# A long convolution with routed experts: channels in four parts of 32, first transform on two row groups, products by halves of a step, z read by whole chunks

## The chip, the cores and the metric

The kernel runs on one core of a Trainium2 chip. What counts is the device time of one execution in microseconds (us). A profile of one execution is at hand, with every instruction, every transfer and the clock that TensorE was granted.

The engines are named as the profile names them: PE (TensorE's products; PEld its weight loads), DVE (VectorE), ACT (ScalarE), POOL (GpSimd) and SP (SyncE, which only issues transfers here). Each engine works through its own instructions in the order in which they were written.

## The reference

For 4 sequences of 11456 positions and 128 channels, `u = x * v` is convolved along the positions with a filter that a small network makes from position vectors. The result times x goes through a layer of eight experts, of which each row that passes a score takes one.

```python
h_filt = (np.maximum(pos_emb @ w1, 0.0) @ w2) * np.exp(-0.01 * pos)[:, None]
Uf, Hf = np.fft.rfft(x * v, n=2 * S, axis=1), np.fft.rfft(h_filt, n=2 * S, axis=0)
x = x * np.fft.irfft(Uf * Hf[None], n=2 * S, axis=1)[:, :S, :]
...
out[do_compute] = xc + gate_w * (np.maximum(xc @ w1[e], 0.0) @ w2[e])
```

## The kernel before

The positions are cut into 3 blocks of 3840 = 60 x 64, and the transform of each block is done in steps of products with fixed matrices, all in float32. Between the steps the data goes to DRAM and comes back in another order. There are three stages.

**Stage 1** (`first_phase`) does the first transform, over 60 positions, for the first half of the channels (64 of 128), and builds the filter's transform beside it. `First.load` (L189) brings a piece of x and one of v in runs of 1 KB, `mult` (L207) multiplies them on DVE, `split` (L211) makes two fp32r halves of the product on ACT and DVE, `data` (L219) multiplies them with c1 in three passes (L204), ACT copies the result out of PSUM (L205), and ACT's queue stores it in `x1d` (L239). Two sets of 60 positions stand below each other on 120 partitions; c1 holds two 120 x 120 matrices, each with zeros in the half that belongs to the other set. `filt` (L244) is a generator whose pieces are woven in; it ends in products with c1f (L290) and in stores to `x1d` from POOL (L298).

**Stage 2** (`freq_phase`) has 60 steps: two halves of channels times 30 steps of 2 frequencies. A step loads `x1` (L397) and its matrices c2 (L395). `filt` (L400) transforms the filter (L403), ACT copies it out (L409), and DVE (L410) and POOL (L411) make combinations of its blocks. `forward` (L414) does the second transform of the data in three blocks (L428, 2 x 256 columns each) and multiplies each out of PSUM with the filter on DVE (L422, six of 1024 elements a step) into y and p; POOL adds these (L424, three of 1024). `back` (L452) takes y of the step two before (`LAG`) through the third transform (L455, six products of 512 columns), ACT copies it to z (L456), and SP stores z in `zd` (L460). After each `back`, `step` (L382) may write a piece of the first transform of the other half of the channels (`second`, L371). In all a step has 3 x 2 x 256 + 2 x 192 + 6 x 512 = 4992 columns on PE without these pieces.

**Stage 3** (`out_phase`) has 32 chunks of 3 blocks. A block loads x (L1049) and its 480 KB of z (L1060) and takes them through the last transform (`product`, L1063). There the two products of one block (L1071) have 64 columns of weights each and write partitions 0 to 63 and 64 to 127. DVE multiplies by x (L1072), and scores, tables and gathers for the experts follow. The rows are gathered into 16 buffers (`XT`), and the experts' products fill PE to the end (`late_slots`).

What sets the order: each stage is written with its schedule fixed, so an engine's order is the order in which the Python code runs. SP issues transfers strictly in that order, and each waits for its buffer and for an earlier transfer that used the same one of eight semaphores.

In the second half of stage 2 `prepare` (L1319) sets up the experts a piece at a time and loads their weights. Its first piece has a copy on DVE of `slotpos` into four buffers (L539) as soon as its load has landed.

Of the kernel before, what the change touches and what calls it, by code (L numbers as in the profile page):

```python
# [20 lines left out]
E, F = 8, 1024  # L21
# [6 lines left out]
DH = D // 2  # L28
# [13 lines left out]
AHEAD = 1  # L42
LEAD = 3
PIECES = 1.2
FSTART = 2
FEND = 2
QX = 4
# [5 lines left out]
ZT = 4  # L53
XT = 16
GATHERS = 12
FETCH = 5
# [17 lines left out]
def tables():  # L74
# [6 lines left out]
    c1 = np.zeros((2, K1, 2, K1, 2))  # L81
    c1f = np.zeros((64, 2, 2, K1, 2))
    for p in range(2):
        c1[p, :, p] = c1f[:K1, p, p] = np.stack([np.cos(th), -np.sin(th)], axis=-1)
# [12 lines left out]
    c3[:64, 1, :64] = -np.sin(ps)  # L97
    c3[64:, 1, :64] = -np.cos(ps)
    c3[:64, 1, 64:] = np.cos(ps)
    c3[64:, 1, 64:] = -np.sin(ps)  # L100
# [37 lines left out]
    winp = winp.transpose(1, 0, 2, 3)  # L138
    return {
        "c1": c1.reshape(2 * K1, 2, 2 * K1).astype(f), "c1f": c1f.reshape(128, 2, 2 * K1).astype(f),  # L140
        "c2": c2.astype(f), "c3": c3.astype(f),
# [14 lines left out]
class First:  # L156


    Q = 4
    STEPS = NB * N2 // (2 * Q)  # L160
    XV, US, XS = 3, 2, 3

    def __init__(self, nc, i, x1d, mc, stage):
        self.nc, self.i, self.x1d = nc, i, x1d
        n = self.Q * B * DH
        at = [0]

        def piece(k):
            at[0] += k * n
            return stage[0:2 * K1, at[0] - k * n:at[0]]  # L170
        self.xv = [[piece(1) for _ in range(self.XV)] for _ in "xv"]
        self.us = [piece(1) for _ in range(self.US)]
        self.xs = [piece(2) for _ in range(self.XS)]
        self.c1 = mc.tile([2 * K1, 2, 2 * K1], F32, name="c1")
        nc.scalar.dma_start(self.c1, i["c1"])
        self.tiles, self.loaded, self.parts = {}, 0, {}

    def halves(self, pool):
        self.c1r = pool.tile([2 * K1, 2, 2, 2 * K1], F32R, name="c1r")
        self.nc.scalar.copy(self.c1r[:, 0], self.c1)  # L180
        self.nc.vector.tensor_tensor(self.c1r[:, 1], self.c1, self.c1r[:, 0].bitcast(F32), ALU.subtract)

    def ahead(self, step):

        while self.loaded < min(step + self.XV, 2 * self.STEPS):
            self.load(self.loaded)
            self.loaded += 1

    def load(self, step):  # L189
        nc, Q = self.nc, self.Q  # L190
        h, r = divmod(step, self.STEPS)
        blk, ch = divmod(r, N2 // (2 * Q))
        self.tiles[step] = []
        for a, nm in enumerate("xv"):
            t = self.xv[a][step % self.XV]
            nc.sync.dma_start(
                t.rearrange("n (q c) -> n q c", q=Q),
                self.i[nm][ch * 2 * Q:(ch + 1) * 2 * Q, :, blk, h].rearrange("(q p) n b d -> (p n) q (b d)", p=2))
            self.tiles[step].append(t)

    def first(self, xs, terms, pool):
        ps = pool.tile([2 * K1, 512], F32, name="ps")
        for a, (c, rhs) in enumerate(terms):
            self.nc.tensor.matmul(ps, c, rhs, start=(a == 0), stop=(a == len(terms) - 1))  # L204
        self.nc.scalar.copy(xs, ps.rearrange("k (q c) -> k q c", c=B * DH))  # L205

    def mult(self, step):  # L207
        if step < 2 * self.STEPS:
            self.nc.vector.tensor_tensor(self.us[step % self.US], *self.tiles.pop(step), ALU.mult)

    def split(self, step, pool):  # L211

        u = self.us[step % self.US]
        ur = pool.tile([2 * K1, 2, self.Q * B * DH], F32R, name="ur")
        self.nc.scalar.copy(ur[:, 0], u)  # L215
        self.nc.vector.tensor_tensor(ur[:, 1], u, ur[:, 0].bitcast(F32), ALU.subtract)
        self.parts[step] = ur

    def data(self, step, pool):  # L219
        nc, Q = self.nc, self.Q  # L220
        h, r = divmod(step, self.STEPS)
        blk, ch = divmod(r, N2 // (2 * Q))
        u = self.us[step % self.US]
        xs = self.xs[step % self.XS]
        n = Q * B * DH
        ur = self.parts.pop(step, None)

        def terms(p, sl):
            if ur is None:
                return (self.c1[:, p, :], u[:, sl]),  # L230
            return [(self.c1r[:, a, p, :], ur[:, b, sl]) for a, b in ((0, 0), (0, 1), (1, 0))]
        for p in range(2):
            for hf in range(n // 512):
                sl = slice(hf * 512, hf * 512 + 512)
                qs = slice(sl.start // (B * DH), sl.stop // (B * DH))
                self.first(xs.rearrange("k (q p c) -> k q p c", q=Q, p=2)[:, qs, p], terms(p, sl), pool)
                if p or hf < n // 512 - 1:
                    yield
        nc.scalar.dma_start(  # L239
            self.x1d[h][:, :, ch * 2 * Q:(ch + 1) * 2 * Q, blk * B * DH:(blk + 1) * B * DH].rearrange("k c m d -> (k c) m d"),  # L240
            xs.rearrange("k (m c) -> k m c", c=B * DH))
        yield
# [1125 lines left out]
```

## Time and profile before

| | us |
|---|---|
| median of three runs | 1756.87 (1756.68 to 1761.15) |
| the profiled execution | 1761.34 |
| its span, first to last instruction | 1759.6 |
| PE busy | 1615.1 (92%) |
| DVE busy | 1269.8 (72%) |
| POOL busy | 1020.3 (58%) |
| ACT busy | 862.7 (49%) |

DMA moved 357.8 MB, 203 GB/s over the span. The mean granted clock of TensorE was 0.969 of full speed.

A busy share is a mean over stages with different limits, so the prediction reads the stages apart. A row of the timeline has start, length, engine, line, operation and tiles; a bracket at its end says how long the engine had been idle and what it was waiting for. float32 products stand there as two records each. A group row (with a bar) has busy time, mean ns of one, and the idle time ahead of it.

### The profile page before, as it was taken

The page shows a single profiled execution, that of the slowest core. Times are in us where ns is not written, and L with a number is a line of the kernel's source. Part 1 is how long each engine was busy: PE and PEld are TensorE (multiplying, and loading weights), DVE is VectorE, ACT ScalarE, POOL GpSimd, SP SyncE. Part 2 cuts the span into 40 slices and gives each one's busy share as a digit, 9 for nine tenths or more (in the row PEclk, how much of TensorE's full clock was granted, in tenths as well). Part 3 has the DMA queues.
Part 4 walks back from the last instruction along what each step waited for, and adds up shares of the span by engine and source line. Part 5 has one row for each costly group of instructions (what it writes and reads, how often), then busy time and mean ns, then how long its engine had stood idle before and what let it go on. Part 6 is the DMA issues. An engine that isn't in the chain of part 4 may idle for free. (4 is left out here: it accounts for less than half of the span.)

```text
span 1759.6 us, 27314 instructions
## 1 busy us (share of the span) xinstructions
PE 1615.1 (92%) x8980; PEld 1121.0 (64%) x8980; DVE 1269.8 (72%) x2404; ACT 862.7 (49%) x1582; POOL 1020.3 (58%) x767
## 2 busy tenths in 40 slices
PE   4989679999999799999567999999998999999996
PEld 2556345555556466655234677777677888888996
DVE  3334359777788799999277778767786777777885
ACT  3655435454454344443133555555544555556773
POOL 1111138677678699999002563632657777776874
PEclk9999889999999899999898999999998999999998
DMA  9999999999998599985999888998831111111110
GB/s 246 304 314 304 299 290 277 305 334 301 338 294 239 160 283 302 276 236 147 214 281 257 223 239 233 247 241 227 232 108 47 31 46 46 44 41 33 36 37 21
DMA packets 255122, 357.80 MB, mean 203 GB/s; under 512 B 24961, under 2 KB 189739, under 8 KB 254979
## 3 DMA queue, kind: packets, MB, share of 16 engines
q1 hardware_dynamic: 187692, 269.74, 53.2%
q10 hardware_dynamic: 47687, 47.71, 8.9%
q0 software_dynamic: 19600, 38.59, 8.4%
q8 instruction: 72, 1.18, 0.3%
q14 instruction: 71, 0.58, 0.1%
HBM read 212.91 MB, written 144.02 MB: 203 GB/s over the span
## 5 line engine op out<-in xcount | busy, mean ns | idle before, releaser
L424 POOL TENSOR_TENSOR y<-y,p 128x1024 f32<-128x1024 f32 x120 | 282.9, 2358 | 101.0 <-DVE y L422 96.3
L455 PE MATMUL zps<-y,c 128*128 128x512 f32 x720 | 339.6, 595 | 0.0
L767 POOL DMA_INDIRECT out<-o,ids x186 | 201.6, 1084 | 178.0 <-DVE o L773 128.5
L703 POOL DMA_INDIRECT xt<-out,ids x186 | 199.1, 1070 | 93.1 <-issue 42.5
L422 DVE TENSOR_TENSOR p<-xp,g 128x1024 f32<-128x1024 f32 x180 | 218.4, 1213 | 44.3 <-PE xp L428 27.0
L422 DVE TENSOR_TENSOR y<-xp,gc 128x1024 f32<-128x1024 f32 x180 | 218.5, 1214 | 20.9 <-PE xp L428 20.9
L428 PEld LDWEIGHTS xp<-x,c 128*128 128x128 f32 x720 | 137.6, 192 | 109.5 <-issue 77.2
L871 DVE SCALAR_TENSOR_TENSOR hh<-hp,hh 128x1024 fp32r<-128x1024 f32 x128 | 155.9, 1218 | 70.5 <-ACT hh L870 70.5
L428 PE MATMUL xp<-x,c 128*128 128x256 f32 x720 | 187.9, 384 | 14.1 <-DVE p L422 14.1
L455 PEld LDWEIGHTS zps<-y,c 128*128 128x128 f32 x720 | 134.9, 191 | 99.9 <-issue 89.7
L456 ACT COPY z<-zps 128x512 f32<-128x512 f32 x180 | 104.0, 587 | 189.2 <-PE zps L455 187.2
L669 POOL DMA_INDIRECT ids<-lists,at x93 | 102.7, 1104 | 134.5 <-DMA out<-xm 93.8
L409 ACT COPY gc<-t 64x384 f32<-64x384 f32 x240 | 113.7, 474 | 135.2 <-DVE y L422 80.1
L870 ACT ACTIVATE hh<-hp 128x1024 fp32r<-128x1024 f32 x128 | 132.1, 1032 | 74.2 <-PE hp L763 74.2
L205 ACT COPY wf<-ps 120x512 f32<-120x512 f32 x192 | 110.4, 591 | 83.4 <-PE ps L204 38.5
L738 DVE TENSOR_TENSOR ws<-wf,ws 128x1024 fp32r<-128x1024 f32 x113 | 137.8, 1220 | 18.1 <-ACT ws L733 11.8
L424 POOL TENSOR_TENSOR p<-p,p 128x1024 f32<-128x1024 f32 x60 | 149.5, 2492 | 0.0
L204 PE MATMUL ps<-ur,c1r 120*120 120x512 f32 x300 | 113.3, 508 | 37.9 <-ACT ur L215 20.4
L1071 PE MATMUL y<-zt,c 120*64 120x512 f32 x384 | 108.4, 643 | 32.0 <-DMA zt<-zd 25.9
L833 PEld LDWEIGHTS bank<-wd,h 128*128 128x128 f32 x928 | 107.8, 191 | 30.9 <-issue 30.8
L761 PE MATMUL hp<-hl,ws 128*128 128x512 f32 (+1 forms) x336 | 122.2, 364 | 2.4 <-DVE hh L871 0.9
L733 ACT CAST ws<-wf 128x1024 fp32r x113 | 117.8, 1043 | 10.4 <-issue 5.1
(194 smaller groups left out, 3330.8 us busy)
## 6 DMA issues: line engine op xcount, KB each, us to landing
x<-x1d SPq DMA_DIRECT2D x60, 960.0 KB
x1d<-wf ACTq DMA_DIRECT2D x48, 960.0 KB
zd<-z SPq DMA_DIRECT2D x120, 384.0 KB
zt<-zd SPq DMA_DIRECT2D x96, 480.0 KB
out<-xm SPq DMA_DIRECT2D x96, 258.0 KB
ox<-xo SPq DMA_DIRECT2D x96, 256.0 KB
wf<-x SPq DMA_DIRECT2D x48, 480.0 KB
wf<-v SPq DMA_DIRECT2D x48, 480.0 KB
```

Source lines behind the costliest of these rows:

```text
L409: nc.scalar.copy(gc[h * 64:(h + 1) * 64, a], t[a * 64:(a + 1) * 64])
L422: nc.vector.tensor_tensor(o, x[:, None].broadcast_to([128, 2, B, D]), v[:, :, None, :].broadcast_to([128, 2, B, D]), ALU.mult)
L424: add = lambda o, v: nc.gpsimd.tensor_tensor(o, o, v, ALU.add)
L428: nc.tensor.matmul(x[:, :, k], c2[:, k], x1[:, k, blk * B:(blk + 1) * B, :], start=True, stop=True)
L455: nc.tensor.matmul(zps, c3[:, a, :], y[:, blk, a], start=(a == 0), stop=(a == 1))
L703: ins = nc.gpsimd.indirect_dma_start(out=xt[:, j], out_offset=None, in_=self.rows[0:have], in_offset=bass.IndirectOffsetOnAxis(ap=ids[:, j ...
L733: nc.scalar.copy(w[:, 0], (self.w1f, self.w2f)[which][:, ds(self.where(nc.scalar, tb), F)])
L738: eng.tensor_tensor(w[:, 1], src[:, ds(self.where(eng, tb), F)], w[:, 0].bitcast(F32), ALU.subtract)
L761: nc.tensor.matmul(hp, w[:, 0, c], hl[:, 0], start=True, stop=False)
L767: ins = nc.gpsimd.indirect_dma_start(out=self.rows, out_offset=bass.IndirectOffsetOnAxis(ap=ids[:, j:j + 1], axis=0), in_=o, in_offset=Non ...
L870: nc.scalar.activation(h[:, 0], hp, AF.Relu)
L871: nc.vector.scalar_tensor_tensor(h[:, 1], hp, 0.0, h[:, 0].bitcast(F32), ALU.max, ALU.subtract)
```

## The change

The channels go in four parts of 32 instead of two halves of 64 (`NP`, `DH`). What follows from that and what is new beside it:

- Stage 1 does the first transform for one part only. The fp32r split is gone. One transfer brings x and v of a piece together, in runs of 6 KB, and a store of x1d writes runs of 6 KB. The two sets of 60 positions now stand on partitions 0 to 59 and 64 to 123 and are multiplied with the same 60 x 120 matrix, as two products of 384 columns with 60 rows each (L215). The filter's products use the same matrix (L267). The filter has a tensor of its own, `x1f`.
- The x1d stores are issued by SP, one step later, and no longer by ACT.
- Stage 2 has 60 steps still: four parts of 15 steps of 4 frequencies. It does the first transform of the other three parts; x times v is on POOL there (L198). A step loads x1 (L381) and the filter (L382) by two transfers. c2 is loaded once and stays.
- The second transform takes data and filter in one product of 480 columns (`spread`, L392), two halves of a step apart, each in its own PSUM tiles. DVE combines the filter out of PSUM (`combine`, L404, L405) and multiplies by halves (`mult`, L412: 1536, 1024 and 512 elements). POOL adds all in two instructions (2048 and 1024 elements, L483, L484). `LAG` is 1 instead of 2.
- z's stores are held back until after the next step's first half. Each run in `zd` has 1536 bytes instead of 3072.
- Stage 3 loads z by whole chunks (1440 KB, two buffers, `ZB`) and x with three buffers; there are 14 row buffers, 4 units of gathers ahead, and 4 buffers h. The row buffers' memsets and the copy of slotpos stand at the start of stage 3.

```diff
-DH = D // 2
+NP = 4
+DH = D // NP
...
-ZT = 4
-XT = 16
+ZT = 3
+ZB = 2
+XT = 14
...
     def mult(self, step):
-        if step < 2 * self.STEPS:
-            self.nc.vector.tensor_tensor(self.us[step % self.US], *self.tiles.pop(step), ALU.mult)
...
+            eng = self.nc.vector if step < self.STEPS else self.nc.gpsimd
+            eng.tensor_tensor(self.us[step % self.US][rows], xv[:, 0], xv[:, 1], ALU.mult)
...
+        for q in range(Q):
+            ps = [pool.tile([2 * K1, 512], F32, name="ps")[:, 0:RUN] for _ in range(2)]
+            for p in range(2):
+                rows = slice(p * 64, p * 64 + K1)
+                nc.tensor.matmul(ps[p], self.c1[rows], u[rows, q * RUN:(q + 1) * RUN], start=True, stop=True)
+            for p in range(2):
+                nc.scalar.copy(xs[:, 2 * q + p], ps[p])
+            if q == 0:
+                self.store()
...
         def step():
-            credit[0] += PIECES
+            n = fi.STEPS * fi.Q
+            credit[0] += (n - LEAD) / (NB * (PER - QX)) if done[0] < n else n / (NB * PER)
...
+            nc.sync.dma_start(x1[:, :, 0:fi.RUN], fi.x1d[h][ks].rearrange("k c n w -> (c n) k w"))
+            nc.sync.dma_start(x1[:, :, fi.RUN:], fi.x1f[ks, :, :, h * w:(h + 1) * w].rearrange("k c n w -> (c n) k w"))
...
+            xp = qpx.tile([128, KH, 512], F32, name=f"xp{j}")
+            for k in range(KH):
+                nc.tensor.matmul(xp[:, k, 0:(NS + NB) * DH], c2(n % PER * KS + j * KH + k), x1[:, j * KH + k], start=True, stop=True)
...
-        LAG = 2
+        LAG = 1
...
+                half(0)
+                combine(n, 1)
+            back(0)
+            begin(n + 1, 0)
+            store()
+            if n < ALL:
+                half(1)
+                del gs[n], xs[n]
+            back(1)
+            if n + 1 < ALL:
+                combine(n + 1, 0)
+            begin(n + 1, 1)
+            if n < ALL:
+                nc.gpsimd.tensor_tensor(y[:, 1:], y[:, 1:], p1, ALU.add)
+                nc.gpsimd.tensor_tensor(y[:, 2:], y[:, 2:], p2, ALU.add)
+            back(2)
...
-            z = ob.tile([2 * K1, 4, BW], F32, name="zt", bufs=ZT)
-            nc.sync.dma_start(z, zs[ch][:, :, blk * BW:(blk + 1) * BW])
+                zts[ch] = ob.tile([2 * K1, 2 * NP, NS * DH], F32, name="zt", bufs=ZB)
+                nc.sync.dma_start(zts[ch], zs[ch])
```

How this moves instructions is seen in the order in which they stand on each engine. On PE, a step in the first half of stage 2 stood like this before (L428 second transform of the data, L403 of the filter, L455 third, L204 first transform of the other half of the channels):

```order
L428 MATMUL xp_2355<-x_2155,c_2153 128x4x64 x2
L403 MATMUL t<-x_2222,c_2220 128x3x64 x2
L455 MATMUL zps<-y,c_61 128x512 x2
L204 MATMUL ps<-wf,c_59 120x512 x2
L428 MATMUL xp_2382<-x_2155,c_2153 128x4x64 x2
L455 MATMUL zps<-y,c_61 128x512 x2
L204 MATMUL ps<-wf,c_59 120x512
L428 MATMUL xp_2396<-x_2155,c_2153 128x4x64 x2
L455 MATMUL zps<-y,c_61 128x512 x2
```

And this is a step of the first part in the changed program (L392 second transform, L423 third, L215 first transform of another part):

```order
L392 MATMUL xp_1340<-x_1182,wf 128x480 x2
L423 MATMUL zps<-y,c_67 128x512 x2
L215 MATMUL ps<-wf,c_65 120x384 x2
L392 MATMUL xp_1363<-x_1182,wf 128x480 x2
L423 MATMUL zps<-y,c_67 128x512 x2
L215 MATMUL ps<-wf,c_65 120x384 x2
L423 MATMUL zps<-y,c_67 128x512 x2
L215 MATMUL ps<-wf,c_65 120x384 x2
```

The third transform and the second one have as many columns as before; the first transform's products come as pairs of 384 columns between them.

On SP, a step of the first half stood like this before (L395 c2, L397 x1, L196 x and v, L460 z; the stores of x1d were on ACT's queue):

```order
L395 DMA c_1889<-c 128x2x128
L397 DMA x_1891<-x1d 128x2x960
L196 DMA wf<-x 120x4x256
L196 DMA wf<-v 120x4x256
L460 DMA zd<-z 64x2x768 x2
```

In the changed program a step of the second part stands like this (L381 x1, L382 the filter, L191 x and v together, L203 the store of x1d, L434 z):

```order
L381 DMA x_2033<-x1d 128x4x384
L382 DMA x_2033<-x1f 128x4x96
L191 DMA wf<-xv 60x1536 x2
L203 DMA x1d<-wf 120x1536
L434 DMA zd<-z 64x4x384 x2
```

The queue has seven transfers a step where it had six, the stores of x1d among them, and their runs are shorter for x1, the filter and z and longer for x, v and x1d.

More of the change, by code (lines that the diff above doesn't have):

```diff
@@ L169, in piece @@
             at[0] += k * n
-            return stage[0:2 * K1, at[0] - k * n:at[0]]
-        self.xv = [[piece(1) for _ in range(self.XV)] for _ in "xv"]
+            return stage[:, at[0] - k * n:at[0]]
+        self.xv = [piece(2).rearrange("n (a c) -> n a c", a=2) for _ in range(self.XV)]
         self.us = [piece(1) for _ in range(self.US)]
-        self.xs = [piece(2) for _ in range(self.XS)]
-        self.c1 = mc.tile([2 * K1, 2, 2 * K1], F32, name="c1")
-        nc.scalar.dma_start(self.c1, i["c1"])
[L176 to L181, printed above, removed]
+        self.xs = [piece(2)[0:2 * K1] for _ in range(self.XS)]
+        self.used = at[0]
+        for xv in self.xv:
+            for rows in (slice(32, 64), slice(96, 128)):
+                nc.vector.memset(xv[rows], 0.0)
+        self.c1 = mc.tile([128, 2 * K1], F32, name="c1")
+        nc.scalar.dma_start(self.c1, i["c1"])
+        self.loaded, self.late = 0, []
     def ahead(self, step):
-        while self.loaded < min(step + self.XV, 2 * self.STEPS):
+        while self.loaded < min(step + self.XV, self.ALL):
             self.load(self.loaded)
@@ L219, in data @@
[L219 to L241, printed above, removed]
+        h, ch = divmod(step, self.STEPS)
@@ L534, in __init__ @@
         nc.sync.dma_start(self.slotpos, i["slotpos"])
-        self.reaches, self.turns = [mc.tile([LP + 1, T2], F16, name=f"reach{k}") for k in range(4)], 0
-        for t in self.reaches:
-            nc.vector.memset(t, 0.0)
-            nc.vector.tensor_copy(t[LP:], self.slotpos[LP:])
         self.counts = mc.tile([E * NS, C], F16, name="counts")
```

360 lines of the change are left out of this document (181 added, 179 removed).

## The prediction

> **What bounds the kernel now.** I first cut the profiled execution into its stages. The columns are the stretch in us, its length, the busy time of PE, PEld, DVE, ACT and POOL (with counts), the granted TensorE clock, the DMA share and GB/s.
>
> ```profile
> 0.00:236.60 236.60, 181.10 (x813) 109.63 (x813) 78.72 (x80) 115.51 (x191) 37.66 (x60) 0.93 0.99 292
> 236.60:536.00 299.40, 294.55 (x901) 168.95 (x902) 234.77 (x209) 146.34 (x272) 212.14 (x106) 0.99 0.99 305
> 536.00:834.70 298.70, 289.01 (x940) 174.88 (x939) 282.82 (x255) 119.43 (x231) 262.02 (x134) 0.98 0.80 235
> 834.70:854.40 19.70, 7.87 (x20) 3.24 (x18) 4.37 (x17) 2.93 (x5) 5.12 (x3) 0.79 0.77 200
> 854.40:950.00 95.60, 66.24 (x531) 30.82 (x532) 60.84 (x229) 27.84 (x91) 4.15 (x4) 0.89 1.04 269
> 950.00:1300.00 350.00, 342.70 (x3094) 252.01 (x3093) 261.21 (x967) 187.75 (x453) 167.59 (x157) 0.99 0.85 227
> 1300.00:1759.60 459.60, 433.62 (x2691) 381.51 (x2690) 347.09 (x651) 262.91 (x339) 331.65 (x305) 0.98 0.15 39
> ```
>
> The first stage (first transform of half the channels, and the filter) is held by DMA: share 0.99, PE idle a quarter of the time. In the second stage PE is full to 98%, first with DMA full beside it, then alone. The third stage is held by DMA for 95 us and by PE after that. So the question is not how busy the kernel is but what each stage is made to wait for.
>
> The timeline gives the price of PE's second stage. Columns are start, length, engine, line, tile.
>
> ```profile
> 441.03 1.03 PE L428 MATMUL xp<-x,c 128*128 128x256 f32 x4
> 441.89 1.88 PE L455 MATMUL zps<-y,c 128*128 128x512 f32 x4
> 443.61 0.59 PE L204 MATMUL ps<-wf,c 120*120 120x512 f32 x1
> ...
> 452.86 1.03 PE L428 MATMUL xp<-x,c 128*128 128x256 f32 x4
> ...
> 689.90 1.03 PE L428 MATMUL xp<-x,c 128*128 128x256 f32 x4
> ...
> 698.29 1.03 PE L428 MATMUL xp<-x,c 128*128 128x256 f32 x4
> ```
>
> Each float32 product stands as two records, so L455's four are two products of 512 columns, 1.72 us from their start to the next line's: 0.86 each. A step without first transform takes 698.29 - 689.90 = 8.39 us, and its 4992 columns at 0.86/512 are 8.39: PE alone sets it. With four first products it takes 452.86 - 441.03 = 11.83, that is 8.39 + 4 x 0.86. Check: 60 x 8.39 + 92 x 0.86 = 582, and one stall, are the 598 us of rows two and three but for 6 us of ramp:
>
> ```profile
> 585.41 0.18 DVE L539 COPY reach<-slotpos 1x128 f16<-1x128 f16 x1 [9.97 <-DMA slotpos<-slotpos]
> 591.75 2.08 PE L428 MATMUL xp<-x,c 128*128 128x256 f32 x4 [9.49 <-DVE p L422]
> ```
>
> **The change, part by part.** *Stage 1: a quarter instead of a half.* What moves is read from the DMA issues (count, KB each).
>
> ```profile
> x<-x1d SPq DMA_DIRECT2D x60, 960.0 KB
> x1d<-wf ACTq DMA_DIRECT2D x48, 960.0 KB
> zd<-z SPq DMA_DIRECT2D x120, 384.0 KB
> ...
> wf<-x SPq DMA_DIRECT2D x48, 480.0 KB
> wf<-v SPq DMA_DIRECT2D x48, 480.0 KB
> x1d<-fx POOLq DMA_DIRECT2D x32, 360.0 KB
> ...
> post<-post POOLq DMA_DIRECT2D x23, 128.0 KB
> ```
>
> A quarter of x and v is 48 x 0.983 / 4 = 11.8 MB, a quarter of x1d's writes another 11.8, the filter's writes stay 11.8, positions 3.1, constants 0.5: 39 MB. The pieces grow from 1 KB to 6 KB, so I take 325 GB/s, between this stage's 292 and the best 50 us below: 120 us. Around it stand 10.3 us until the first product of x and v, 4.9 us from the issue of the first x1 load to its first matmul, and 4 us (an estimate, from that same 4.9) for the last store to land:
>
> ```profile
> 10.31 1.23 DVE L209 TENSOR_TENSOR wf<-wf 120x1024 f32<-120x1024 f32 x1 [4.40 <-DMA wf<-v]
> ...
> 231.66 0.40 SPq L397 DMA_DIRECT2D x<-x1d  x1
> ...
> 236.60 1.65 PE L403 MATMUL t<-x,c 128*128 128x192 f32 x4 [6.03 <-DMA x<-x1d]
> ```
>
> Together 139 instead of 236.6. The dropped fp32r split (L215, L216) was on ACT and DVE, which are not the bound; the six new memsets are covered by the wait for the first load.
>
> *The first transform on row groups.* No row shows products that share PE by rows; products that share it by columns (L1071, 64 wide) do stand there:
>
> ```profile
> 1102.13 1.08 PE L1071 MATMUL y<-zt,c 120*64 120x512 f32 x4
> ...
> 1103.14 0.39 PE L761 MATMUL mh<-hl,ws 128*128 128x256 f32 x1
> ```
>
> Two products of 512 columns cost 1.01 us to the next line's start, not 1.72, so they run side by side, 0.15 over one product's 0.86. A pair of 384 columns is then 0.64 + 0.15 + 0.10 (an estimate for entering, from the same 0.15) = 0.89 us; one after the other it would be 1.29 + 0.15 = 1.44. I take 0.89 and keep 1.44 as a rival. The Trainium skill (TensorEngine Tiling (Array Packing), Tiling Modes) speaks against interleaving such pairs with full-size products: changing the tiling mode drains the engine. The 0.15 agrees; by a drain that costs nothing the 92 pairs of stage 2 would take 92 x 0.25 = 23 us less.
>
> *Stage 2 on PE.* L392 has 4 x 480 columns and L423 6 x 512 a step: the same 4992, so 8.39 us. Of 96 pairs 4 run before the first x1 arrives; 28 come in the first 12 steps (2.55 a step: 8.39 + 2.27 = 10.7 us), 64 in the next 30 (2.13: 10.3 us), and 18 steps have none.
>
> *Stage 2 on DMA.* A step loads 0.98 MB of x1 and stores 0.79 of z; a whole step of the first transform (two pairs) moves 1.47. In the first 12 steps that is 0.98 + 0.79 + 1.27 x 1.47 + 0.26 of c2 (128 x 512 float32) = 3.9 MB, later 3.3. The highest load that the trace shows held for long:
>
> ```profile
> 300.00:500.00 200.00, 199.87 (x611) 112.45 (x611) 149.59 (x138) 100.99 (x187) 137.98 (x70) 1.00 1.02 323
> GB/s 368 273 282 284 283 305 379 230 376 329 336 363 358 291 234 379 367 320 350 269 333 336 247 365 299 294 307 268 331 360 267 369 331 370 360 337 313 294 379 373
> 450.00:500.00 50.00, 50.00 (x154) 28.14 (x153) 37.14 (x36) 26.26 (x49) 33.08 (x18) 1.00 1.03 339
> ```
>
> PE never waited there, so 323 is a demand that was met, not a ceiling, but at share 1.02 not much is left. 3.3 MB in 10.3 us is 324 GB/s: met. 3.9 MB in 10.7 us is 366, above every 50 us here: at 340 the first 12 steps take 11.5 us each. Pieces of x1 and z shrink (3840 to 1536 and 384 bytes; 3072 to 1536) while x, v and x1d pieces grow; I let these cancel.
>
> *Stage 2 on DVE and POOL.*
>
> ```profile
> 690.09 1.21 DVE L422 TENSOR_TENSOR p<-xp,g 128x1024 f32<-128x1024 f32 x1
> 691.22 1.21 DVE L422 TENSOR_TENSOR y<-xp,gc 128x1024 f32<-128x1024 f32 x1
> ...
> L773 DVE SCALAR_TENSOR_TENSOR o<-mto,xt 128x128 f32<-128x128 f32 x128 | 36.5, 335 | 4.9 <-PE mto L895 4.9
> ...
> L424 POOL TENSOR_TENSOR y<-y,p 128x1024 f32<-128x1024 f32 x120 | 282.9, 2358 | 101.0 <-DVE y L422 96.3
> ...
> L411 POOL TENSOR_TENSOR g<-gc 128x256 f32<-128x256 f32 x60 | 50.6, 843 | 54.5 <-ACT gc L409 54.5
> ```
>
> DVE keeps 6144 product elements a step, 6 x 1.13 = 6.8 us, and gets four small ops (L404, L405) at 0.3, by L773's row: 8.0 us, just under 8.39. POOL: from 843 and 2358 ns one element costs 1.97 ns over 0.34 us, so 2048 cost 4.4, 1024 cost 2.4, and the products of x and v that come to it (768) 1.85: 8.7 us a step, under 10.3. Behind POOL's two adds stand only L423's second and third products of the step after, a whole step later, so that wait is covered; the cover is gone only if a product of x and v at POOL's head waits for a late load. SP's queue takes the x1d stores too; it stands for the last copies at three part borders, while x1 is loaded three steps ahead. I allow 8.5 us for the last 15 steps, where DVE is nearly level with PE.
>
> Sum: 12 x 11.5 + 30 x 10.3 + 3 x 8.4 + 15 x 8.5 = 600, ramp 6 as before. The 9.5 us stall goes: slotpos is now read at the start of the third stage, where DVE waits anyway. Then the end of the stage:
>
> ```profile
> 833.49 1.21 DVE L422 TENSOR_TENSOR y<-xp,gc 128x1024 f32<-128x1024 f32 x1
> ...
> 854.40 1.97 PE L1071 MATMUL y<-zt,c 120*64 120x512 f32 x4 [11.83 <-DMA zt<-zd]
> ```
>
> From the last product to L1071 it was 19.7 us (834.7 to 854.4); now it is two adds on POOL (6.8), a product and a copy (2.5), the 11.8 us that PE waited for z, and 3 for the larger first z (1.0 MB more at 323 GB/s): 24. The first product of the third stage stands at 139 + 606 + 24 = 769 instead of 854.4: 85 us earlier.
>
> *Stage 3.* z by chunks moves the same bytes in 12 KB pieces instead of 1 KB. What it can take away:
>
> ```profile
> PE y L1071 <- DMA zt<-zd: 25.9, 12, 11.8
> ```
>
> 11.8 of it is the start, counted above, so 14 remain, and a row at 269 GB/s that could rise. I take 10 (bounds 0 and 20, the excess of 95.6 us over PE's 66 less what chains of small ops need). The fewer buffers (XT, FETCH, h) I cost at nothing: gathers still run four units ahead of a PE that is full.
>
> Total: 1759.6 - 85 - 10 = 1665 of span, 1666 with the 1.7 us around it; the profiled run (1761.3) stood 4.5 above the median 1756.9, so **1662 us**.
>
> **Rivals.** *Rows one after the other* (0.12): pairs at 1.44 us make 12 x 12.1 + 30 x 11.5 + 25 + 128 = 643; stage 1 then is PE's, 24 x (1.2 + 1.9) + 32 x 1.44 + 12 x 0.86 = 131 + 19 = 150. Its 1.2 is this:
>
> ```profile
> 104.05 1.30 PE L309 MATMUL fa<-fw,h 128*64 128x128 f32 x16
> 105.28 1.65 PE L204 MATMUL ps<-ur,c1r 120*120 120x512 f32 x6
> ```
>
> First product of the third stage at 150 + 643 + 30 = 823, total 1715. Against it: L1071's 1.01. *DMA somewhat slower* (0.14), since x1's filter part comes in pieces of 384 bytes that cost more than their share: at 300 GB/s, between the rows' 292 and 305, the 191 MB of stage 1 and the first 45 steps (39 + 12 x 3.9 + 30 x 3.34 + 3 x 1.8) take 637 us, first product at 637 + 19 + 128 + 30 = 814, total 1706. The Trainium skill (DMA: Bandwidth & Descriptors, Specifications) has transfers under 512 B read, modified and written; if each of those pieces counts twice, the 9 MB of them in the first 45 steps add 28 us, 1690 in all, and no run so far shows it.
> *DMA much slower, so slower than before* (0.07): if pieces of 1536 bytes and less run as the z reads of 854 to 950 did, at 269, 191 MB take 710 us, first product at 887, no gain after it: 1789. It decides from 278 GB/s down, where 191 / 0.278 + 177 = 864 eats all. Against it: x1's pieces lie one behind the other in memory. *Nothing limits but PE* (0.06): 10.7 in the first steps, 360 GB/s in stage 1, 20 in stage 3: 1630.
>
> **How the numbers follow.** The forecast has 0.61. The range, 1625 to 1720, takes in all but the much slower DMA and the tails. Faster by over 0.3% (5 us, about what a measurement can tell from no change) is 0.93, slower 0.05, the same 0.02, around that rival's turning point.
>
> **What would show it.** First L392 near 139 us; two L215 products starting together and 0.9 us to the next line; steps of 11.5, 10.3 and 8.5 us; first L1071 near 769; no 9 us gap after the fourth part begins. Wrong it is if PE waits for x1 in the first 45 steps, if L215 pairs stand one after the other, or if POOL's adds are what L423 waits for.

## The result, and the profile after

The changed kernel took 1716.36 us (median of 4 runs, 1713.97 to 1721.88) against 1756.78 before: a ratio of 0.9758 as recorded (the quotient of the two medians is 0.9770), 95% interval 0.9732 to 0.9785. It is faster, as forecast, but by 40 us where 95 were forecast (1662). The ratios here leave out two executions, over 1.5% above the fastest of their kernel: one of the kernel before, and the one of border, below, from whose profile its stages are read. The profiled execution took 1714.62 us, of which 1712.8 are the span.

First the stages of the changed kernel (stretch, length, busy time of PE, PEld, DVE, ACT, POOL with counts, granted clock, DMA share, GB/s). They are cut at the first L392, at the first product of the third stage (L1074, L1071 before) and behind the first eight chunks of z:

```profile
0.00:161.90 161.90, 110.77 (x649) 58.50 (x649) 39.44 (x48) 63.92 (x133) 26.56 (x47) 0.88 0.83 264
161.90:790.00 628.10, 604.93 (x1570) 248.31 (x1571) 493.70 (x636) 286.93 (x724) 494.02 (x167) 0.98 0.95 301
790.00:893.00 103.00, 71.63 (x487) 31.11 (x487) 52.66 (x197) 25.20 (x82) 1.68 (x2) 0.75 0.85 216
893.00:1712.80 819.80, 782.27 (x5831) 635.35 (x5827) 617.17 (x1649) 454.10 (x801) 507.51 (x464) 0.99 0.46 122
```

The kernel before, cut in the same places of its third stage:

```profile
854.40:938.00 83.60, 60.55 (x487) 27.63 (x489) 52.30 (x196) 24.66 (x82) 1.12 (x1) 0.91 1.04 267
938.00:1759.60 821.60, 782.01 (x5827) 636.71 (x5827) 616.85 (x1650) 453.84 (x801) 502.27 (x464) 0.98 0.46 123
```

| stretch, us | before | forecast | after | after less forecast |
|---|---|---|---|---|
| stage 1, to the first L392 | 236.6 | 139 | 161.9 | +23 |
| stage 2, to the first product of the third | 617.8 | 630 | 628.1 | -2 |
| third stage, to the end | 905.2 | 895 | 922.8 | +28 |
| span | 1759.6 | 1665 | 1712.8 | +48 |

The other 6 us of the miss are the step from span to median: the profiled run was taken as 4.5 us above the median, as the old one was; the new one lies 1.7 below. The gain stands in stage 1 alone (75 us); stage 2 gave back 10 and the first eight chunks of the third 19. Behind those chunks the two kernels are alike within 2 us.

Stage 2 is as long as it was forecast, and PE sets it, as can be seen in its timeline around 450 us (start, length, line, tiles; each float32 product is two records):

```profile
442.23 0.91 PE L215 MATMUL ps<-wf,c 60*120 60x384 f32 x4
443.07 1.88 PE L392 MATMUL xp<-x,c 128*128 128x480 f32 x4
444.78 3.60 PE L423 MATMUL zps<-y,c 128*128 128x512 f32 x8
448.31 0.91 PE L215 MATMUL ps<-wf,c 60*120 60x384 f32 x4
449.15 1.88 PE L392 MATMUL xp<-x,c 128*128 128x480 f32 x4
450.86 1.88 PE L423 MATMUL zps<-y,c 128*128 128x512 f32 x4
452.67 0.91 PE L215 MATMUL ps<-wf,c 60*120 60x384 f32 x4
```

A pair of L215 takes 0.84 us to the next line, too little for two products of 384 columns in a row (1.29), and no product in these rows waits for anything. The whole step is PE's, with DMA full beside it:

```profile
200.00:300.00 100.00, 100.00 (x276) 39.37 (x275) 73.90 (x92) 51.70 (x129) 82.53 (x31) 1.00 1.02 346
```

What stands beside a pair is 0.1 us longer on either side: L423's two products take 1.81 us ahead of a pair (450.86 to 452.67) instead of 1.72, L392's two 1.71 behind one instead of 1.61. So a pair costs 0.84 + 0.2 = 1.04 us in a step. This is the place at which the Trainium skill (TensorEngine Tiling (Array Packing), Tiling Modes) has the engine drain for a new tiling mode; the trace agrees, with 0.2 us a pair.

In stage 1, PE waits in front of the filter's first products (L259) for their positions:

```profile
29.40 1.98 PE L259 MATMUL fa<-post,fw 128*128 128x512 f32 x4
37.58 2.04 PE L259 MATMUL fa<-post,fw 128*128 128x512 f32 x2 [6.20 <-DMA post<-post]
39.55 1.64 PE L215 MATMUL ps<-wf,c 60*120 60x384 f32 x4
...
48.73 1.13 PE L259 MATMUL fa<-post,fw 128*128 128x512 f32 x2
55.92 2.05 PE L259 MATMUL fa<-post,fw 128*128 128x512 f32 x2 [6.06 <-DMA post<-post]
57.89 1.64 PE L215 MATMUL ps<-wf,c 60*120 60x384 f32 x4
```

The pairs L215 stand behind those products on PE, so they wait too, and with them the stores of x1d and the next loads. Cutting stage 1 shows it:

```profile
47.00:60.00 13.00, 6.94 (x21) 2.24 (x21) 0.00 (x0) 3.63 (x8) 0.58 (x2) 0.69 0.49 123
...
60.00:137.00 77.00, 71.23 (x550) 43.03 (x546) 25.08 (x34) 39.23 (x83) 7.31 (x14) 0.94 0.89 301
141.00:154.00 13.00, 6.03 (x17) 2.17 (x16) 0.00 (x0) 4.21 (x11) 2.35 (x2) 0.75 0.91 314
```

From 47 to 60 us DMA moves 123 GB/s; from 60 to 137 PE is busy for 71 of 77 us; and from 141, when the first quarter's products are done, the queues still work for 13 us before the first x1 can be read. On PE that end looks like this (the first row is the first quarter's last two pairs, with one of their eight records missing; what stands between it and L392 are the second quarter's four pairs that run ahead):

```profile
139.52 1.67 PE L215 MATMUL ps<-wf,c 60*120 60x384 f32 x7
141.61 0.91 PE L215 MATMUL ps<-wf,c 60*120 60x384 f32 x4 [0.42 <-POOL wf L198]
...
161.89 6.48 PE L392 MATMUL xp<-x,wf 128*128 128x480 f32 x8 [9.85 <-DMA x<-x1f]
```

In the third stage the views are SP's issues and DVE's products around one chunk:

```profile
837.89 0.39 SPq L1055 DMA_DIRECT2D zt<-zd  x1
838.38 0.35 SPq L1049 DMA_DIRECT2D ox<-xo  x1
...
842.24 0.33 SPq L1049 DMA_DIRECT2D ox<-xo  x1
849.95 0.34 SPq L1079 DMA_DIRECT2D out<-xm  x1
...
841.52 0.69 DVE L1075 TENSOR_TENSOR xm<-y,ox 128x512 f32<-128x512 f32 x1 [1.40 <-PE y L1074]
848.59 0.69 DVE L1075 TENSOR_TENSOR xm<-y,ox 128x512 f32<-128x512 f32 x1 [3.37 <-DMA ox<-xo]
...
849.34 1.08 PE L1074 MATMUL y<-zt,c 120*64 120x512 f32 x4 [3.62 <-DVE xm L1075]
851.97 1.98 PE L1074 MATMUL y<-zt,c 120*64 120x512 f32 x4
```

An ox of 256 KB, issued 0.5 us behind a z of 1440 KB (838.38 behind 837.89), is what DVE gets only at 848.6, 10 us after its issue. The PSUM bank of y stays taken until then, PE waits for the bank (3.62 us), and SP, which has the output's store next in its order, issues nothing from 842.6 to 849.9: so DMA is first full and then idle in each chunk (share 0.85, before 1.04). Over the eight chunks:

```profile
DVE xm L1075 <- DMA ox<-xo: 28.2, 7, 6.4
PEld y L1074 <- DVE xm L1075: 24.1, 8, 5.6
```

### The profile page after: what moved, and what is told of

The parts are those of the page before. It is cut to its first block, busy times and chain, and to the rows that moved or that the text cites. A ratio compares the mean times of both kernels' runs of the same rounds, so it can differ in the third digit from the quotient of the medians.

```text
span 1712.8 us, 26697 instructions
## 1 busy us (share of the span) xinstructions
PE 1569.6 (92%) x8528; PEld 973.3 (57%) x8528; DVE 1203.0 (70%) x2529; ACT 830.2 (48%) x1740; POOL 1029.8 (60%) x679
## 5 line engine op out<-in xcount | busy, mean ns | idle before, releaser
L423 PE MATMUL zps<-y,c 128*128 128x512 f32 x720 | 337.2, 597 | 1.8 <-POOL y L483 1.4
L483 POOL TENSOR_TENSOR y<-y,p 128x2048 f32<-128x2048 f32 x60 | 271.6, 4527 | 82.5 <-DVE p L412 81.7
L767 POOL DMA_INDIRECT out<-o,ids x186 | 206.4, 1110 | 169.4 <-DVE o L773 122.9
L423 PEld LDWEIGHTS zps<-y,c 128*128 128x128 f32 x720 | 134.2, 190 | 171.3 <-issue 154.8
L412 DVE TENSOR_TENSOR p<-xp,g 128x1024 f32<-128x1024 f32 x240 | 217.4, 947 | 0.0
L412 DVE TENSOR_TENSOR y<-xp,g 128x1536 f32<-128x1536 f32 x120 | 210.7, 1756 | 4.1
L1074 PE MATMUL y<-zt,c 120*64 120x512 f32 x384 | 116.9, 690 | 48.3 <-DVE xm L1075 22.8
L215 PE MATMUL ps<-wf,c 60*120 60x384 f32 x512 | 123.4, 553 | 25.7 <-DVE wf L198 13.6
L484 POOL TENSOR_TENSOR y<-y,p 128x1024 f32<-128x1024 f32 x60 | 141.6, 2360 | 4.7
L1075 DVE TENSOR_TENSOR xm<-y,ox 128x512 f32<-128x512 f32 x96 | 66.2, 689 | 106.9 <-DMA ox<-xo 51.8
L217 ACT COPY wf<-ps 120x384 f32<-120x384 f32 x256 | 109.9, 485 | 57.7 <-PE ps L215 52.3
L392 PE MATMUL xp<-x,wf 128*128 128x480 f32 x256 | 122.7, 604 | 13.6 <-DMA x<-x1f 9.9
L404 DVE TENSOR_TENSOR g<-xp,g 128x128 f32<-128x128 f32 x120 | 34.7, 289 | 131.9 <-ACT g L397 131.8
```

The source lines that it names most:

```text
L215: nc.tensor.matmul(ps[p], self.c1[rows], u[rows, q * RUN:(q + 1) * RUN], start=True, stop=True)
L392: nc.tensor.matmul(xp[:, k, 0:(NS + NB) * DH], c2(n % PER * KS + j * KH + k), x1[:, j * KH + k], start=True, stop=True)
L412: nc.vector.tensor_tensor(o[:, :, :, j * KH:(j + 1) * KH].rearrange("p s a k b d -> p (s a) k b d"), x[:, None].broadcast_to([128, m, KH, ...
L423: nc.tensor.matmul(zps, c3[:, a, :], y[:, blk, a], start=(a == 0), stop=(a == 1))
L483: nc.gpsimd.tensor_tensor(y[:, 1:], y[:, 1:], p1, ALU.add)
L484: nc.gpsimd.tensor_tensor(y[:, 2:], y[:, 2:], p2, ALU.add)
```

## The experiments

The columns show the place of the first L392, that of the first product of the third stage, and the length of its first eight chunks, all from the profiled execution. Five profiles whose stage 1 is the changed kernel's have the first L392 between 161.9 and 163.7. The first batch ran where the kernel before took 1760 us; in the later ones it took 1928 to 1952, and what made them longer lies behind the eight chunks (the changed kernel itself has 162.8, 790.3 and 103.0 there, and 538.5 us instead of 461.3 behind its last product). So ratios are read inside a batch, and stages across them.

| kernel | us | before, same batch | ratio (95%) | L392 | product | 8 chunks |
|---|---|---|---|---|---|---|
| before | 1756.78 | | | 236.6 | 854.4 | 83.5 |
| changed | 1716.36 | 1756.78 | 0.9758 (0.9732 to 0.9785) | 161.9 | 790.0 | 103.0 |
| ox_first | 1698.14 | 1759.66 | 0.9640 (0.9609 to 0.9670) | 162.9 | 790.3 | 87.8 |
| posts12 | 1710.32 | 1759.66 | 0.9715 (0.9673 to 0.9756) | 153.7 | 781.2 | 103.8 |
| rows_serial | 1780.51 | 1759.66 | 1.0116 (1.0083 to 1.0150) | 166.8 | 817.1 | 103.5 |
| before_zchunk | 1819.38 | 1759.66 | 1.0328 (1.0295 to 1.0360) | 233.1 | 854.3 | 104.3 |
| ox_four | 1847.04 | 1928.20 | 0.9540 (0.9488 to 0.9593) | 163.7 | 792.5 | 88.2 |
| border | 1866.59 | 1928.20 | 0.9641 (0.9592 to 0.9691) | 156.6 | 787.8 | 102.6 |
| rows_serial2 | 1900.18 | 1928.20 | 0.9839 (0.9796 to 0.9882) | 168.2 | 819.0 | 102.7 |
| before_zchunk2 | 1933.68 | 1928.20 | 1.0024 (0.9995 to 1.0052) | 236.0 | 857.8 | 104.4 |
| z_act | 1866.30 | 1937.96 | 0.9642 (0.9607 to 0.9678) | 161.9 | 791.4 | 92.5 |
| both | 1848.33 | 1937.96 | 0.9529 (0.9494 to 0.9564) | 151.8 | 779.6 | 86.7 |
| both_act | 1859.15 | 1937.96 | 0.9608 (0.9565 to 0.9650) | 152.0 | 779.6 | 92.1 |
| all_three | 1839.09 | 1937.96 | 0.9495 (0.9451 to 0.9539) | 148.1 | 779.4 | 88.1 |
| after_again | 1881.54 | 1952.12 | 0.9651 (0.9588 to 0.9714) | 162.8 | 790.3 | 103.0 |
| all_three_again | 1862.63 | 1952.12 | 0.9531 (0.9449 to 0.9612) | 148.5 | 780.5 | 90.1 |
| four | 1852.82 | 1952.12 | 0.9518 (0.9449 to 0.9587) | 143.3 | 774.6 | 90.5 |

rows_serial, before_zchunk and ox_four have fewer than 14 xt buffers (the gathered rows). By the code, the experts' last part (`late_slots`) holds seven units of two such buffers at a time, so with fewer it works on other rows than the reference's; these three are read only up to the last product of the third stage, and their totals say nothing of the change.

**The order of ox and z (ox_first).**

```diff
             product(ch, blk)
+            load(NB * ch + blk + ZT - 1)
             if blk == NB - 1:
                 load_z(ch + ZB)
-            load(NB * ch + blk + ZT - 1)
```

> The changed kernel, with the load of the next ox issued ahead of the load of the chunk of z after next instead of behind it. Theory A (an ox load is queued behind each 1.44 MB load of z and lands some 9 us after its issue, PE then waits for the DVE product that waits for ox): the first eight chunks of the third stage take about 11 us each instead of 13.0, and the total is about 1702 us. Rival B (the DMA queue is full of z in pieces of 12 KB whatever the order): the chunks stay at 13 us, total 1713 to 1720.

The eight chunks as one row of stretches, in the run with the order turned:

```profile
790.30:878.00 87.70, 63.98 (x485) 28.48 (x485) 51.08 (x195) 24.82 (x83) 1.11 (x1) 0.86 0.97 254
```

15 us of the 19 that the chunks had lost come back with the order of two statements, and 18 in the total (1698.1, 1702 expected). DMA moves 254 GB/s instead of 216 with the same bytes, and DVE's waits for ox fall from 28.2 us to 18.6, not to nothing. Theory A holds.

**ox further ahead (ox_four), and z on another queue (z_act).** The first has `ZT = 4` and `XT = 12`; the second this:

```diff
-                nc.sync.dma_start(zts[ch], zs[ch])
+                nc.scalar.dma_start(zts[ch], zs[ch])
```

> The changed kernel, with ox loaded three blocks ahead into four buffers instead of two ahead into three; two xt buffers fewer make the room. Theory A (ox lands too late behind z): the first eight chunks of the third stage take 88 us or less instead of 103, as with the two loads swapped, and the first product of the third stage stays near 790. Rival B (what counts is only that ox is issued behind z, not how far ahead): the eight chunks stay above 97 us. Rival C, for the last stage alone: with two xt buffers fewer the stretch behind the last product of the third stage gets longer than its 461 us, as it did by 38 us in the two runs with one fewer.

> The changed kernel, with the loads of z in the third stage issued by ACT on its own DMA queue, the order of ox and all else as it was. Theory A (ox waits since it stands behind z in one queue): the first eight chunks take 84 to 92 us instead of 103 and the ratio to the kernel before is about 0.967. Rival B (z in pieces of 12 KB takes the DMA engines themselves, so that ox is as late from another queue): the eight chunks stay above 98 us, ratio about 0.976.

ox_four: 88.2, where theory A had 88 or less and rival B over 97; rival C stays open, since the last stretch works on other rows there. z_act, where z goes through another queue than ox, as a row of stretches, and then from its list of waits:

```profile
791.40:883.90 92.50, 69.22 (x485) 30.27 (x485) 52.04 (x196) 25.00 (x82) 1.11 (x1) 0.80 0.90 235
```

```profile
DVE xm L1075 <- DMA ox<-xo: 21.4, 6, 5.3
```

92.5 stands just beyond the 92 that theory A allowed, and away from rival B's 98. Two thirds of what the order wins (10.5 of 15) come with the queue alone; the waits for ox get fewer and shorter, not none. The Trainium skill (DMA: Bandwidth & Descriptors, Queues, rings and completion order) has each DMA engine take turns between the queues it has work for; the trace agrees, by these 10.5 us. The ratios expected here and below were reckoned from the first batch and can't be set against those of the later ones.

**Whole chunks of z in the kernel before (before_zchunk, before_zchunk2).** ZT = 3, ZB = 2, `load_z` as in the change; the first with 13 xt buffers, the second with 14 and one lt fewer.

> The kernel before, with only this part of the change: z loaded by whole chunks into two buffers, ox three deep, and one or two buffers fewer of xt, h and o's gathers to make room. Theory A (whole chunks are what costs the third stage): the first eight chunks take about 13 us instead of 10.2 and the total is about 1775 us. Rival B (the third stage is longer for another reason that came with the four parts): the first eight chunks stay near 10.2 us, total 1752 to 1760.

> As before_zchunk, with room made by one buffer fewer of lt, so that xt has 14. Theory A: the first eight chunks of the third stage take 104 us against the 83.5 of the kernel before, the last stretch 463 us as before, total 1778 us. Rival B (the longer chunks are given back later, where PE is the bound): total 1757 to 1763.

The eight chunks of the second as a row of stretches, and what DVE waits for in them by the list of waits:

```profile
857.80:962.20 104.40, 72.50 (x485) 31.02 (x485) 52.57 (x196) 25.18 (x82) 2.10 (x2) 0.75 0.84 215
```

```profile
DVE xm L1076 <- DMA ox<-xo: 27.7, 7, 6.1
```

This one part, put into the kernel before with the fewer buffers that make its room, makes the same 104 us with the same share (0.84), rate (215) and waits for ox (27.7) as the changed kernel: it is the cause of the longer eight chunks, and the four parts of channels are not. The total was a miss, though. before_zchunk is 26 us behind the kernel before at the last product (1321.7 against 1295.8), as it should be, but before_zchunk2's ratio is 1.0024 and not 1.012, which by the total alone is rival B's case. In that batch two stretches, from the eight chunks to the last product and behind it, are each 70 to 90 us longer than in the first, for every kernel, and vary by some 15 from profile to profile; no profile of the kernel before was taken in that batch, so whether the 20 us are given back there stays open. Where the kernel before takes 1760 us they were not, as before_zchunk's 26 us say; and behind the eight chunks the changed kernel, ox_first and the kernel before are alike within 4 us.

**Positions further ahead (posts12).**

```diff
-            pt = fp.tile([128, P], F32, name="post", bufs=4)
+            pt = fp.tile([128, P], F32, name="post", bufs=16)
...
-        posts = [positions(*pc) for pc in pieces[:3]]
+        posts = [positions(*pc) for pc in pieces[:12]]
...
-            if n + 3 < len(pieces):
-                posts.append(positions(*pieces[n + 3]))
+            if n + 12 < len(pieces):
+                posts.append(positions(*pieces[n + 12]))
```

> The changed kernel, with the filter's positions loaded 12 pieces ahead into 16 buffers instead of 3 ahead into 4. Theory A (between 20 and 60 us of the first stage PE stands 13 us for positions, and the first transform behind it on PE with it): those waits go, L259 ends near 45 us instead of 58, the first L392 stands near 148 instead of 162, total about 1702 us. Rival B (the first stage is bound by its bytes on the DMA queues, and the positions only take turns with them): the first L392 stays at 158 to 162, total 1712 to 1720.

PE's timeline of that run begins the filter like this:

```profile
32.00 3.75 PE L259 MATMUL fa<-post,fw 128*128 128x512 f32 x4 [5.40 <-DMA fw<-w]
35.69 1.64 PE L215 MATMUL ps<-wf,c 60*120 60x384 f32 x4
37.25 3.10 PE L259 MATMUL fa<-post,fw 128*128 128x512 f32 x6
```

The waits for positions are gone, and 8.2 us of stage 1 with them; 5.4 us now go to the filter's weights, which land later the more pieces are issued ahead of them: the first L259 stands at 25.3 us with three pieces ahead, 28.8 with six (both) and 32.0 with twelve. They are most of what is missing to the expected 14; the total, 6 us less, is within the spread of these runs (1703.8 to 1715.6) of what the stage says.

**The end of stage 1 (border).** No x or v of the second quarter before the first x1 loads, LEAD = 0:

```diff
-        while self.loaded < min(step + self.XV, self.ALL):
+        while self.loaded < min(step + self.XV, self.ALL if step >= self.STEPS else self.STEPS):
...
+            fi.ahead(fi.STEPS)
             fi.mult(fi.STEPS)
```

> The changed kernel, with no load of x and v of the second quarter before the loads of the first x1, and with none of the four pairs that ran ahead of the first L392 (they run later, in steps). Theory A (at the end of the first stage the DMA queues still have 13 us of transfers when PE is done with the first quarter, and 3.6 MB of those, 11 us at 325 GB/s, belong to the second quarter): the first L392 stands at 150 to 155 instead of 162; four pairs at 1.035 us come to the second stage, total about 1709 us. Rival B (the last store of x1 and the filter would land as late without them): the first L392 stays at 159 or later, total 1716 to 1724.

It came out between the two: the first L392 at 156.6, 5 us earlier, not 7 to 12, and the first twelve steps were 3.9 us longer for the four pairs. So the loads of the second quarter are about 5 of the 12 us by which this border is over its forecast; set against both, all_three gives 3.7 for the same part (151.8 to 148.1). For the rest only the issues speak, no run: the last pairs and the filter's last pieces end together, so that some 2.9 MB of the first quarter's and the filter's own stores (four of 720 KB) are issued within 6 us, from 138.5 on.

**Pairs on all rows, one product after the other (rows_serial, rows_serial2).**

```diff
-                rows = slice(p * 64, p * 64 + K1)
-                nc.tensor.matmul(ps[p], self.c1[rows], u
+                rows = slice(0, 64 + K1)
+                nc.tensor.matmul(ps[p], self.cz[rows, p], u
```

> The changed kernel, with the first transform's two products of a pair on all rows, one after the other: each has a table whose other half of the rows is zero (one xt buffer fewer makes the room). Theory A (a pair on two row groups runs side by side and costs 1.035 us in a step, since 10.44 us with two pairs less 8.37 without is 2.07): on all rows a pair costs 768 columns at 0.86 / 512, 1.29 us, a step with two pairs takes 10.95 us, the second stage is 92 x 0.255 = 23 us longer, total about 1740 us. Rival B (the pair ran one after the other already, which is what the total of 1715 us of that rival in the prediction would say): the steps stay at 10.44 or come down, total 1705 to 1718.

> As rows_serial, with room made by one buffer fewer of lt and by leaving out the first table of which the new one is a copy, so that xt keeps its 14. Theory A: the steps with two pairs take 10.96 us as in rows_serial, and the last stretch, behind the last product of the third stage, is 461 us again: total 1739 us. Rival B (the 38 us that rows_serial had behind the last product come from the pairs): total 1775 to 1782.

PE in rows_serial2:

```profile
444.04 1.46 PE L217 MATMUL ps<-wf,cz 124*120 124x384 f32 x4
445.34 1.88 PE L425 MATMUL zps<-y,c 128*128 128x512 f32 x4
447.05 1.46 PE L217 MATMUL ps<-wf,cz 124*120 124x384 f32 x4
448.35 1.77 PE L394 MATMUL xp<-x,c 128*128 128x480 f32 x4
449.96 1.88 PE L425 MATMUL zps<-y,c 128*128 128x512 f32 x4
```

A pair takes 1.30 us here, and its neighbours have their 1.71 and 1.61 again. A step with two pairs is 10.96 us in both runs (10.95 expected), the second stage 22 to 23 us longer, stage 1 about another 5. The row groups are worth 27 to 29 us up to the third stage (817.1 and 819.0 against 790.0). That stage 1 gets longer at all with longer products says that PE, too, is on its path. The 38 us behind the last product don't come from the pairs: with 14 xt buffers rows_serial2 has 541.5 us there, beside 538.5 of the changed kernel in such a batch. The total of 1739 can't be compared with a run of that batch; the ratio is 0.9839, beside 0.9651 for the changed kernel in another slow batch.

**Repairs together (both, all_three, four).** both is ox_first with 6 positions ahead in 8 buffers; all_three adds border; four also loads the first z ahead of the last transform's matrices (c4) and ox:

```diff
+        load_z(0)
         ahead = [load_x(q) for q in range(ZT - 1)]
-        for ch in range(ZB):
+        for ch in range(1, ZB):
             load_z(ch)
```

> The changed kernel with two repairs: ox issued ahead of z, and the filter's positions loaded 6 pieces ahead into 8 buffers (posts12 with half the lead, so that the filter's weights, for which PE stood 5.4 us there, aren't behind twelve pieces). If the gains are in stages that follow one another they add: the first L392 at about 152, the first eight chunks 88 us, ratio to the kernel before 0.964 less 9 / 1757, about 0.959. Rival (what the first stage wins is waited for again in the second or third): ratio 0.963 to 0.965.

> As the one with two repairs, and x and v of the second quarter loaded only after the first x1, as in border. Theory A (the first stage's 23 us over the forecast are the positions' 8, the second quarter's loads' 5, and the rest of start and PE): the first L392 at about 146, the first twelve steps 4 us longer, ratio about 0.958. Rival B (without the wait for positions the second quarter's loads find room on the queues earlier): the first L392 stays at 151 or later, ratio 0.960 or more.

> The changed kernel as it is, on the chip of this batch, to be set against the two below. If the chip is like the first: 1716 us, ratio 0.976. If it is like the one on which the kernel before took 1928 to 1938 us: the same first L392 (162), first product (790) and eight chunks (103), and a ratio of 0.965 to 0.975, that is, 28 to 32 us behind the version with three repairs, which had 779.4 and 88.1.

> The version with three repairs again, beside the changed kernel itself. Theory A (the first stage's positions and early loads and the third stage's ox behind z are what the change gave away): 26 us less than the changed kernel on the same chip, by 10.6 us at the first product and 15 in the eight chunks. Rival B (later stages give some of it back): 20 us or less between them.

> The version with three repairs, with the first chunk of z loaded ahead of c4 and the first two ox, not behind them, at the start of the third stage. Theory A (0.63 MB ahead of it on the queue make the first product late, by the 2.7 us that they take at 230 GB/s): the first product stands near 776.5 instead of 779.4, ox is there as early as it is needed, and the total is 2 to 3 us less. Rival B (z waits for the last store to land, and the others are through before it): the first product stays at 779.

The stages add: both has the first L392 at 151.8, its eight chunks at 86.7, all_three 148.1 (146 by theory A, 151 or later by rival B) and 88.1; the four pairs that border puts into the steps take its gain away again at the first product (779.4 against 779.6). On one batch all_three is 18.9 us less than the changed kernel, not 26, which is rival B's 20 or less: but up to the end of the eight chunks it is 22.7 us ahead (9.8 and 12.9), and the rest is within what the later stretches vary there, so theory and rival aren't told apart by the total. four was wrong: from its first L392 to its first product it takes 631.3 us, as all_three does (631.3 and 632.0); its earlier product comes from a stage 1 of 143.3, whose code is the same, so that a first L392 can differ by 5 us between two profiles of one code. SP issues the first z 620.8 us after the first L392 in four and 620.7 in all_three: it waits for the last store, and what all_three issues ahead of it is through by then, as rival B had it.

And both with z on ACT's queue besides:

> As the one with two repairs, and z issued by ACT. Theory A (order and queue are two ways to the same thing): the first eight chunks take 84 to 89 us, no more than 3 us less than with the order alone, ratio 0.957 to 0.960. Rival B (a z load on ACT holds up ACT's copies behind it): the eight chunks take over 92 us.

Its eight chunks take 92.1 us and its ratio is 0.9608, as rival B had it: with z issued by ACT the order no longer helps, and 86.7 became 92.1. That ACT's copies are held up, as rival B says, isn't shown: in the eight chunks DVE waits 19.2 us for ox (17.4 in both) and PE 15.4 for DVE, and no wait for a copy of ACT is among the longest.

The version to keep is ox_first's order, at 0.9640 of the kernel before where the changed one has 0.9758; with the positions six ahead it is 0.9529 in one of the slower batches, where the changed kernel has 0.9651 in another. all_three has 0.9495 beside that 0.9529, with intervals that overlap and the first product at the same place, so what border adds isn't shown.

## Why the prediction was right in its sign and wrong in its size

- **Stage 1 taken as DMA's, 39 MB at 325 GB/s: the first step that failed.** It was forecast from bytes and a rate alone. The bytes were 42.8 MB, not 39 (264 GB/s over 161.9 us), since the second quarter's first x and v and the first x1 are loaded ahead of its end; and the rate was not DMA's alone to set, for the order on PE holds the pairs behind the filter's positions (8 to 10 us, posts12 and both), and PE is nearly full behind them (71 of 77 us): 128.6 us instead of 120 (12.6 to 141.2). The allowance of 9 us between the last pair and the first L392 was 20.7 (141.2 to 161.9): about 4 to 5 for the second quarter's loads (border, all_three), the others only argued above. 2 us more went to the first product of x and v (12.6 instead of 10.3). In the kernel before, 237 us of DMA had covered all of it; cut the bytes from 69 MB to 43, and what had been under them is next. What the first stage still has over 139 with all three repairs (9 us in all_three, 4 in four) stays open.
- **z by whole chunks, "I take 10 (bounds 0 and 20)": the second step that failed, by sign.** No reason was given for excluding a loss, and the measured value is 19.5 the other way. The wait for z that was to shrink did go; a new one for ox took its place (28.2 us of DVE's time, with ox 10 us from issue to use). The working counted z's pieces and not what stands behind them in the queue; ox_first, which turns only that order, brings 15 of the 19 us back.
- **A pair at 0.89 us** was 1.04 (0.84 and 0.2 beside it); 92 x 0.15 = 14 us. **The first twelve steps at 11.5 us**, DMA's rate, were 10.7: PE set them. The prediction's 2.55 pairs a step don't fit its own 28 pairs in 12 steps (2.33); 26 ran there, so a step moved 3.6 MB and not 3.9, at 338 GB/s. The two errors, 14 us too little and 10 too much, nearly cancel, so that stage 2 was right to 2 us partly by luck. Later steps (10.4 to 11.4 and 8.37), the absent 9.5 us stall and the last stretch (28.7 us for 24) were close.
- **The rivals.** The rival of rows one after the other had 1715 us, and the time was 1716.4, yet the rows run side by side: a time that fits is no evidence for the mechanism; 442.23 to 443.07 is, and rows_serial2, where a pair one after the other takes 1.30 us. Slower DMA (300 and 269 GB/s) didn't come about; PE waited for x1 only ahead of the first L392, so these runs don't show what pieces of 384 bytes would cost.

## What to carry to other kernels

A stage that is held by bytes hides chains: when its bytes are cut, read which engine's order holds it next (here PE waiting in order for a four-deep buffer), not only the bytes left over the best rate. A transfer made larger is a longer wait for whatever is issued behind it in its queue; put the small and urgent one first, or give it more lead, before counting what larger pieces save. And a bound of zero on a cost or gain needs a reason of its own.

## What the hardware showed that was not expected

The same products of the third stage's eight chunks (x485 to x487) kept PE busy for 60.6 us at a granted clock of 0.91 (before), 64.0 at 0.86 (ox_first), 69.2 at 0.80 (z_act) and 71.6 at 0.75 (changed). So waits of 3 to 6 us go with a second cost: 11 us more of busy time for the same products. A single line shows it: the four records of L1074 that end a wait of 3.62 us at 849.34 took 1.08 us, and the next four, at 851.97, 1.98. The granted clock is 1.00 from 849.3 to 850.5 and 0.50 from 851.9 to 853.9: here it falls about 1.3 us after the end of the wait (at 850.6), not in it. The Trainium skill (TensorE: Matmul & The Clock Gate, Part 1) has the clock halve after an idle window of about 3.4 us; the trace agrees in kind, with waits of 3.6 us and a ratio of 1.8.

Pieces of 12 KB brought no higher rate: while z of whole chunks is loaded DMA is full and slow,

```profile
839.00:845.00 6.00, 6.00 (x35) 2.52 (x36) 4.09 (x18) 1.84 (x8) 0.00 (x0) 0.60 1.05 233
846.00:849.50 3.50, 0.16 (x2) 0.16 (x4) 0.87 (x3) 0.27 (x3) 0.00 (x0) 1.00 0.92 288
```

233 GB/s at a share of 1.05, and 288 right behind it for ox and the stores of the output, in pieces of 2 KB.
